# A fused attention and expert kernel whose hand-listed order of operations and loads is computed anew

## The chip, the cores and the metric

The kernel runs on one core of one Trainium2 chip. The metric is the device time of one execution in microseconds (us), as the median of several runs.

## What is computed

Eight batches of attention, eight heads each, 576 queries against 16 beacon keys and 576 causal keys of width 64, and then a gated feed-forward over the 4608 tokens that come out:

```python
scores = scale * np.matmul(q, k_all.transpose(0, 1, 3, 2))
scores = np.where(causal, -1000000000.0, scores)
...
x = np.ascontiguousarray(attn_out.transpose(0, 2, 1, 3)).reshape(B * S, H * D)
...
h = a * b @ w3          # a = x @ w1, b = x @ w2
return (h @ w_out).astype(np.float32)
```

Inputs and output are float32; the kernel works in float16 with float32 sums.

## The kernel before

There is no scheduler in the program. The string ORDER (L62 to L266) lists some 1,890 operations, and the last lines of the kernel walk through it and issue each one:

```python
for line in ORDER.split(";"):
    kind, *args = line.split()
    ops[kind](*(int(arg) if arg.isdigit() else arg for arg in args))
```

So the string sets the order in which each engine and each DMA queue gets its instructions, which PSUM bank an operation takes (its last numbers), whether DVE (D) or ACT (A) makes a copy, and which queue stores a result (P: GpSimd's, S: SyncE's). Each engine works its own instructions in order; between engines the semaphores of the program's tiles decide.

The names in ORDER, by stage. `b` is a batch, `t` a pair of heads, `c` a chunk of 128 rows.

- Loads. For batch 0, `lq` and `lk` (L396, SyncE's queue) bring q and k as float32 into the staging tiles `st`; for the others `lq` (L377), `lk` (L385) and `lv` (L385) bring chunks of q, k and v on GpSimd's queue, with a cast to float16; `lkb` (L410) and `lvb` (L418) bring the beacon rows. `l1`, `l2` (L423) load the first two expert weights into `w`, `l3` (L432) rows of the third into `st`, `lo` (L435) the output weight into `wo`.
- Transposes. For batches 0 to 2 (and with `x` for the attention outputs of batches 0 and 1) PE transposes (`tq`, `tk`, L451 and L457; `x`, L592). From batch 3 on `Dq` (L500) and `Dk` (L506) do it by a DMA on SyncE's queue, and so does `TX` (L601) for the attention output from batch 2 on: it writes xT from x.
- Attention. `s` (L535) makes a group of score blocks, `exp` (L545, ACT) their exponentials in `ring`, `m` (L555, DVE) the causal mask, `v` (L566) the product with the values, `n` (L577, L578, DVE) the division by the sum, into x.
- Fold of two weights. `t3` (L513) and `f` (L520) make Wt = w3 times w_out, `ew` copies it from PSUM. It is done once, between batch 0 and batch 1.
- Expert. Tokens of batch 0 go through plain products `a`, `b` (L660). For the other batches seven products `p` (L649) stand for the eight of a two by two block product; `S` (L618) are the sums of the halves of xT that they need and `T` (L631) those of the weights, on DVE. `ce`, `c1` (ACT, L678, L681), `u`, `t1`, `t2`, `g1`, `g2` (DVE, L684 to L698) put the products together and multiply a by b into gT.
- Output. `o` (L704) multiplies gT by Wt, `eo` (L358 on ACT, L360 on DVE) scales the sum into a staging tile `st`, and `st` (L717) stores it. There are eight staging tiles, so an `eo` waits until the earlier store from its tile has landed.

While the products of one batch run, the scores of the next but one are prepared. A sum S of a batch waits until the five transposes TX of that batch have landed; they wait for the last `n` of the batch. A load into a buffer waits for the last reader two batches earlier.

Of the kernel before, what the change touches and what calls it, by code (L numbers as in the profile page):

```python
# [68 lines left out]
cast 0 3 k; s 0 6 0; l1 1; m 0 1 1; tk 0 3 7; exp 0 6 0; cast 0 3 q; s 0 7 2; lq 1 4 P; m 0 0 1;
tq 0 3 6; exp 0 7 2; l1 0; eq 0 3 D 6; v 0 0 1 5; l3 1; ek 0 3 A 7; v 0 0 0 4; m 0 1 0;  # L70
n 0 0 1 5; l3 6; s 0 8 0; v 0 1 0 7; exp 0 8 0; l2 1; n 0 0 0 4; s 0 10 2; m 0 2 0; s 0 9 4;
exp 0 10 2; s 0 11 0; m 0 2 1; l2 0; v 0 1 1 6; n 0 1 0 7; exp 0 9 4; s 0 12 2; l2 3; n 0 1 1 6;
v 0 2 1 7; exp 0 11 0; m 0 3 0; t3 0 6; n 0 2 1 7; l1 2; v 0 2 0 5; exp 0 12 2; v 0 3 0 4;
m 0 3 1; tq 1 4 7; l1 3; n 0 2 0 5; e3 0 A 6 0; v 0 3 1 3; n 0 3 0 4; lq 1 3 P; tq 1 0 5;
n 0 3 1 3; x 0 0 4; x 0 4 6; tk 1 3 2; ex 0 0 A 4; eq 1 4 D 7; x 0 1 3; ex 0 4 A 6; l2 2;
x 0 3 1; ex 0 1 D 3; x 0 2 7; ex 0 3 A 1; t3 1 6; ex 0 2 D 7; a 0 3 1 7; lo 0; a 0 1 1 4;
a 0 3 0 3; ea 0 1 1 A 4 1; lo 1; b 0 3 0 1; ea 0 3 0 D 3 2; b 0 3 1 4; ea 0 3 1 D 7 0; a 0 0 0 3;
g 0 3 1 4 0; lk 1 4 P; b 0 0 0 7; T 1 1; ea 0 0 0 A 3 3; g 0 3 0 1 2; a 0 1 0 4; ek 1 3 A 2;
g 0 0 0 7 3; a 0 2 1 3; lk 1 2 P; T 0 1; ea 0 1 0 A 4 0; b 0 1 1 7; ea 0 2 1 A 3 2; a 0 2 0 4;
e3 1 A 6 1; g 0 1 1 7 1; lk 1 0 P; b 0 2 1 3; T 1 2; ea 0 2 0 A 4 3; b 0 2 0 7; b 0 1 0 6;  # L80
# [718 lines left out]
```

## Time and profile before

| what | us |
|---|---|
| median of 3 runs | 294.33 |
| all runs | 293.73, 297.48, 294.33 |
| the profiled execution, its own time | 293.03 |
| its span, first to last instruction | 291.3 |

The rows further down come from the one profiled execution. Times in them are microseconds from the span's start. PE is TensorE's matmul, PEld its weight load, DVE VectorE, ACT ScalarE, POOL GpSimd, SP SyncE; SPq is SyncE's sequencer, which issues DMAs. A line such as L649 is a line of the kernel.

### The profile page before, as it was taken

What the parts mean: (1) busy time and instruction counts of PE and PEld (TensorE: products, weight loads), DVE (VectorE), ACT (ScalarE), POOL (GpSimd) and SP (SyncE); (2) the same over time, 40 slices, a digit from 0 to 9 for tenths busy, and PEclk for the clock granted to TensorE, in tenths of its full rate; (3) what the DMA queues carried; (4) which work ended last, traced back from release to release, by engine and by line L of the source; (5) the groups of instructions that cost most, each with busy time, mean ns of one, the idle gap of its engine ahead of it and who ended that gap; (6) DMA issues with size and microseconds to landing.
All of it is one profiled execution on the core that took longest, in us unless ns stands there. A gap on an engine that the chain in (4) does not pass through costs nothing.

```text
span 291.3 us, 8145 instructions
## 1 busy us (share of the span) xinstructions
PE 276.5 (95%) x3204; PEld 185.4 (64%) x3204; DVE 227.7 (78%) x605; ACT 172.7 (59%) x272; POOL 133.5 (46%) x185
## 2 busy tenths in 40 slices
PE   6799999999999999998969998999999999999994
PEld 2478776657576756765647645775776667766751
DVE  5786785666799958996669867998899788997970
ACT  2686335857886489257954388434848886424313
POOL 8496696995982602959314570583500021002000
PEclk9579999999999999999999999999999999999999
DMA  7999999999999994999999999999992163602004
GB/s 199 205 186 199 187 170 182 174 143 128 108 145 134 115 128 81 170 160 177 175 148 115 157 140 227 73 134 184 218 192 44 40 146 104 124 2 108 38 0 180
DMA packets 156549, 40.33 MB, mean 138 GB/s; under 512 B 146208, under 2 KB 152864, under 8 KB 156512
## 3 DMA queue, kind: packets, MB, share of 16 engines
q0 software_dynamic: 114384, 26.62, 104.8%
q1 hardware_dynamic: 42128, 13.20, 28.9%
q8 instruction: 25, 0.41, 0.6%
q14 instruction: 12, 0.10, 0.1%
HBM read 39.32 MB, written 9.44 MB: 167 GB/s over the span
## 4 chain that ended last, share of the span: by engine, by line
PE 78%; DMA 10%; DVE 5%; POOL 2%; issue 2%; SPq 1%; ACT 1%; DVEq 0%; POOLq 0%; ACTq 0%
PE ps L649 30%; PE ps L704 17%; PE ps L535 8%; PE ps L566 8%; PE ps L660 5%; PE ps L520 5%; DMA xT<-x 3%; DMA out_dram<-st 3%; DMA kT<-k 2%; DMA b<-in_beacon_k_dram 2%; PE ps L457 1%; DVE x L578 1%; POOL q L377 1%; PE ps L451 1%; PE ps L513 1%
## 5 line engine op out<-in xcount | busy, mean ns | idle before, releaser
L545 ACT ACTIVATE ring<-ps 128x1024 f16<-128x1024 f32 x104 | 101.5, 1024 | 25.7 <-PE ps L535 24.0
L704 PE MATMUL ps<-Wt,gT 128*128 128x512 f16 x288 | 77.4, 380 | 0.0
L649 PEld LDWEIGHTS <-w 128*128 128x128 f16 x448 | 42.6, 98 | 17.7 <-issue 1.4
L678 ACT COPY es<-ps 128x288 f32<-128x288 f32 x56 | 22.2, 400 | 45.1 <-PE ps L649 39.4
L717 POOL DMA_DIRECT2D out_dram<-st x31 | 17.6, 577 | 62.8 <-ACT st L358 26.4
L649 PE MATMUL ps<-S,T 128*128 128x288 f16 x224 | 42.0, 286 | 2.3 <-DVE x L578 2.3
L649 PE MATMUL ps<-xT,w 128*128 128x288 f16 x224 | 43.0, 286 | 0.0
L649 PE MATMUL ps<-S,w 128*128 128x288 f16 x224 | 42.4, 286 | 0.2 <-DVE gT L698 0.2
L566 PEld LDWEIGHTS <-ring 128*128 128x128 f16 x960 | 35.5, 99 | 10.3 <-issue 2.2
L649 PEld LDWEIGHTS <-T 128*128 128x128 f16 x336 | 31.5, 98 | 15.3 <-issue 3.3
L566 PE MATMUL ps<-va,ring 128*128 128x65 f16 x960 | 38.9, 195 | 1.5 <-DMA va<-in_v_dram 1.3
L385 POOL DMA_DIRECT2D va<-in_v_dram x40 | 34.5, 871 | 12.4 <-PE ps L704 10.3
L535 PE MATMUL ps<-qT,kT 64*128 64x80 f16 (+4 forms) x736 | 36.2, 232 | 3.3 <-DVE kT L354 1.4
L385 POOL DMA_DIRECT2D k<-in_k_dram x35 | 30.0, 870 | 19.9 <-DMA kT<-k 10.0
L377 POOL DMA_DIRECT2D q<-in_q_dram x35 | 30.4, 878 | 16.3 <-DMA qT<-q 13.5
L704 PEld LDWEIGHTS <-gT 128*128 128x128 f16 x288 | 25.2, 98 | 18.4 <-issue 3.1
L535 PEld LDWEIGHTS <-kT 64*128 64x128 f16 x736 | 20.8, 97 | 21.5 <-issue 16.5
L578 DVE TENSOR_TENSOR x<-ps,rd 128x256 f16<-128x256 f32 (+1 forms) x64 | 31.4, 491 | 2.2
L698 DVE TENSOR_TENSOR gT<-ps,es 128x288 f16<-128x288 f32 x64 | 28.5, 451 | 4.7 <-PE ps L649 2.6
L684 DVE TENSOR_TENSOR us<-ps,es 128x288 f32<-128x288 f32 x56 | 25.1, 452 | 3.6 <-PE ps L649 3.0
L681 ACT COPY ps<-ps 128x288 f32<-128x288 f32 x56 | 21.3, 384 | 10.8 <-PE ps L649 8.1
L687 DVE TENSOR_TENSOR us<-ps,us 128x288 f32<-128x288 f32 x56 | 24.6, 451 | 2.8 <-PE ps L649 1.5
(69 smaller groups left out, 318.3 us busy)
## 6 DMA issues: line engine op xcount, KB each, us to landing
out_dram<-st POOLq DMA_DIRECT2D x31, 256.0 KB, 6.8
q<-in_q_dram POOLq DMA_DIRECT2D x28, 128.0 KB, 6.5
va<-in_v_dram POOLq DMA_DIRECT2D x24, 128.0 KB, 6.9
k<-in_k_dram POOLq DMA_DIRECT2D x21, 128.0 KB, 5.9
st<-in_moe_w_dram POOLq DMA_DIRECT2D x8, 256.0 KB, 7.0
w<-in_moe_w_dram POOLq DMA_DIRECT2D x8, 256.0 KB, 9.2
out_dram<-st SPq DMA_DIRECT2D x5, 256.0 KB, 2.3
st<-in_q_dram SPq DMA_DIRECT2D x4, 288.0 KB, 6.6
```

The costliest lines, as they stand in the source:

```text
L377: nc.gpsimd.dma_start(dst[:rows, c], src[b, :, ds(c * P, rows), :].rearrange("h s d -> s h d"))
L385: nc.gpsimd.dma_start(dst[ds(p0, rows), c], src[b, :, ds(s0, rows), :].rearrange("h s d -> s h d"))
L535: nc.tensor.matmul(pair(n)[:, hh, ds(col, w)], kT[ds(hh * 64, 64), t, ts(jt, P)], qT[ds(hh * 64, 64), t, ds(q0, w)],)
L545: nc.scalar.activation(held(b, g)[:, :, 0:GW], pair(n), AF.Exp, scale=scale)
L566: nc.tensor.matmul(pv[:, 2 * at + hh, 0 : D + 1], held(b, g)[:, hh, ds(col, P)], va[:, jt, 2 * t + hh, 0 : D + 1], start=(jt == 0), stop=( ...
L578: nc.vector.tensor_tensor(x16s[b % NB2][:, ds(2 * h, ni), ts(t, P)].rearrange("p i (h d) -> p i h d", h=2), pv[:, 0 : 2 * ni, 0:D].rearran ...
L649: nc.tensor.matmul(half(n), sta[:, j], mov[:, j], start=(j == 0 and i in (1, 3, 5)), stop=(j == 1), skip_group_check=True,)
L678: nc.scalar.copy(es[i], half(n))
L684: nc.vector.tensor_tensor(us[j], half(n), es[i], ALU.add)
L687: nc.vector.tensor_tensor(us[j], half(n), us[j], ALU.add)
L698: nc.vector.tensor_tensor(gT[:, kf, ds((2 * b + 1) % 4 * HT, HT)], half(n), es[i], ALU.mult)
L704: nc.tensor.matmul(bank(n), gT[:, kf, ds(i * P % NG2, P)], Wt[:, kf, :], start=(kf == 0), stop=(kf == NFT - 1),)
```

## The change

Only ORDER changes: all of its lines are written anew. Every kind of operation occurs as often as before (392 `p`, 144 `o`, 104 `s`, 64 `v`, 30 `TX`, 25 `Dq`, 25 `Dk`, 36 stores, of them 31 on GpSimd's queue), and no tile and no function is touched. PE and the two queues issue as many instructions as before; between DVE and ACT some copies change sides: 17 of the 36 `eo` are on DVE in place of 12, and 12 of the 28 copies of transposed q and k in place of 19. The fold moves up: 12 of the 32 `f` and 4 of the 8 `t3` now stand ahead of the first expert product of batch 0, where there were 2 `t3` and no `f`; the three `tq` and `tk` of batch 1 that stood there move behind it. The first lines below are around the transposes TX of batch 3, the others around the fold.

```diff
-st 4 P 4; m 4 1 0; o 10 1 0; TX 3 3; t2 1 0; exp 4 0 2; v 4 1 0 4; st 2 P 2; m 4 0 1; p 2 6 4 1;
-s 4 5 6; n 4 1 0 4; TX 3 1; s 4 7 2; exp 4 5 6; o 10 2 0; g2 2 6 1 0; m 4 0 0; o 9 3 5;
...
+exp 0 4 2; tq 0 3 1; t3 0 0; l3 1; exp 0 3 4; s 0 5 2; l3 6; exp 0 5 2; tk 0 3 5; m 0 1 0;
+e3 0 D 0 0; lo 1; ek 0 3 A 5; eq 0 3 D 1; l1 1; exp 0 7 6; v 0 0 1 0; m 0 2 0; m 0 1 1; lo 2;
...
+c1 0 6; o 9 2 1; TX 3 2; g2 2 5 4 1; p 2 7 4 5; p 2 6 6 6; g2 2 7 5 3; p 2 6 3 4; o 11 0 2;
+u 6 2 0; TX 3 4; o 11 1 2; t1 4 0; p 2 6 2 0; s 4 6 4; Dk 5 3; g1 2 6 0 0; o 10 2 7; exp 4 6 4;
```

Three places, as the engines' instructions stand. First SyncE's queue at the five transposes TX of batch 3 (xT_59 from x_1_78; qT_72 and kT_74 belong to batch 4, qT_73 and kT_75 to batch 5). Before:

```order
L506 DMA_TRANSPOSE kT_74<-k_0_68 128x4x128
L601 DMA_TRANSPOSE xT_59<-x_1_78 128x4x112
L601 DMA_TRANSPOSE xT_59<-x_1_78 128x4x80
L601 DMA_TRANSPOSE xT_59<-x_1_78 128x4x128 x3
L500 DMA_TRANSPOSE qT_73<-q_1_67 128x4x64
L500 DMA_TRANSPOSE qT_73<-q_1_67 128x4x128 x3
L506 DMA_TRANSPOSE kT_75<-k_1_69 128x4x128 x3
```

The five stood behind all transposes of batch 4 and ahead of those of batch 5. After:

```order
L506 DMA_TRANSPOSE kT_74<-k_0_68 128x4x128 x2
L601 DMA_TRANSPOSE xT_59<-x_1_78 128x4x128
L506 DMA_TRANSPOSE kT_74<-k_0_68 128x4x80
L601 DMA_TRANSPOSE xT_59<-x_1_78 128x4x128
L500 DMA_TRANSPOSE qT_72<-q_0_66 128x4x128
L601 DMA_TRANSPOSE xT_59<-x_1_78 128x4x112
L601 DMA_TRANSPOSE xT_59<-x_1_78 128x4x128
L601 DMA_TRANSPOSE xT_59<-x_1_78 128x4x80
L506 DMA_TRANSPOSE kT_75<-k_1_69 128x4x128
```

The last two transposes of batch 4 have moved between the first ones of x. Second, GpSimd's queue at the same place. Before, with 15 loads and stores listed between the first TX of batch 3 and the last (va is v, st the output staging tiles), its end:

```order
L377 DMA q_0_66<-in_q_dram 128x8x64 x2
L385 DMA va_71<-in_v_dram 128x8x64 x2
L717 DMA out_dram<-st_91 128x512
L717 DMA out_dram<-st_89 128x512
L410 DMA k_1_69<-in_beacon_k_dram 16x8x64
```

The store from st_89 stood between the third and the fourth TX. After, the five TX of batch 3 all stand between the first row here and the second, with no load or store listed between them:

```order
L385 DMA va_70<-in_v_dram 128x8x64
L717 DMA out_dram<-st_91 128x512
L385 DMA k_1_69<-in_k_dram 128x8x64
L385 DMA k_0_68<-in_k_dram 128x8x64 x2
L377 DMA q_1_67<-in_q_dram 128x8x64
```

The loads of batches 5 and 6 stand behind the transposes where they stood among them. Third, GpSimd's queue in the opening (st there is a row block of w3, wo the output weight, w the first two expert weights). Before:

```order
L385 DMA va_70<-in_v_dram 80x8x64
L377 DMA q_1_67<-in_q_dram 128x8x64
L432 DMA st_87<-in_moe_w_dram 128x1024
L385 DMA k_1_69<-in_k_dram 128x8x64
L423 DMA w_62<-in_moe_w_dram 128x4x256
L377 DMA q_1_67<-in_q_dram 64x8x64
L423 DMA w_62<-in_moe_w_dram 128x4x256
```

Here w stood ahead of wo, which followed behind all eight loads of w. After:

```order
L385 DMA va_70<-in_v_dram 128x8x64
L432 DMA st_87<-in_moe_w_dram 128x1024
L385 DMA va_70<-in_v_dram 128x8x64
L385 DMA va_70<-in_v_dram 112x8x64
L418 DMA va_70<-in_beacon_v_dram 16x8x64
L385 DMA va_70<-in_v_dram 128x8x64
L385 DMA va_70<-in_v_dram 80x8x64
L432 DMA st_89<-in_moe_w_dram 128x1024
L435 DMA wo_65<-in_moe_w_out_dram 128x2x512
```

One block of w3 has moved in behind the first chunk of batch 0's v, and wo ahead of w.

## Rows read from the trace of the kernel before

**Rows 1.** The page: span and busy time of the engines.

```profile
span 291.3 us, 8145 instructions
PE 276.5 (95%) x3204; PEld 185.4 (64%) x3204; DVE 227.7 (78%) x605; ACT 172.7 (59%) x272; POOL 133.5 (46%) x185
```

**Rows 2.** Stretches of 10 us: length, each engine's busy time (instructions), granted clock, DMA.

```profile
core 0: us, PE busy (x) PEld busy (x) DVE busy (x) ACT busy (x) POOL busy (x), PEclk, DMA share, GB/s
130.00:140.00 10.00, 9.08 (x123) 5.47 (x121) 6.54 (x19) 7.45 (x10) 10.00 (x14) 1.00 2.31 162
140.00:150.00 10.00, 7.67 (x129) 4.74 (x128) 5.90 (x16) 7.46 (x10) 0.61 (x2) 1.00 1.69 169
170.00:180.00 10.00, 8.62 (x141) 5.16 (x141) 5.96 (x16) 8.99 (x11) 3.58 (x6) 1.00 2.15 195
```

**Rows 3.** PE in order of time: start, length, instructions, [idle before <- releaser].

```profile
136.05 0.30 PE L566 MATMUL ps<-va,ring 128*128 128x65 f16 x4
136.61 0.19 PE L566 MATMUL ps<-va,ring 128*128 128x65 f16 x1 [0.26 <-DMA va<-in_v_dram]
137.45 0.37 PE L566 MATMUL ps<-va,ring 128*128 128x65 f16 x7 [0.66 <-DMA va<-in_v_dram]
...
149.37 0.41 PE L649 MATMUL ps<-S,T 128*128 128x288 f16 x2 [2.33 <-DVE x L578]
...
172.52 0.54 PE L566 MATMUL ps<-va,ring 128*128 128x65 f16 x12 [0.35 <-DMA va<-in_v_dram]
...
179.82 0.60 PE L535 MATMUL ps<-qT,kT 64*128 64x112 f16 x15 [1.02 <-DVE st L360]
```

**Rows 4.** The chain that ended last, pieces with their lengths.

```profile
139.09 8.95 DMA xT<-x
149.23 0.82 DVE S L618 x2
...
170.92 8.06 DMA out_dram<-st
179.08 0.70 DVE st L360
```

**Rows 5.** GpSimd's queue, 122 to 150 us, in order of time.

```profile
128.16 2.31 POOL L385 DMA_DIRECT2D k<-in_k_dram x3 [3.02 <-DMA kT<-k]
...
131.34 1.79 POOL L385 DMA_DIRECT2D va<-in_v_dram x2
...
139.39 1.22 POOL L717 DMA_DIRECT2D out_dram<-st x2
```

**Rows 6.** Issues of DMA, 130 to 150 us: median us to landing.

```profile
out_dram<-st POOLq DMA_DIRECT2D x3, 256.0 KB, 7.7
xT<-x SPq DMA_TRANSPOSE x3, 7.2
```

**Rows 7.** The same view of 222 to 256 us.

```profile
out_dram<-st POOLq DMA_DIRECT2D x7, 256.0 KB, 3.2
xT<-x SPq DMA_TRANSPOSE x10, 3.2
```

**Rows 8.** Line L601, the transposes TX, over the whole span.

```profile
DMA to landing us min/median/max: 2.3/4.4/9.6
```

**Rows 9.** The fold's group by line: count | busy us, mean ns of one.

```profile
L520 PE MATMUL ps<-wo,wT 128*128 128x512 f16 x64 | 16.8, 380 | 0.0
```

**Rows 10.** The opening in stretches, columns as in rows 2.

```profile
5.00:9.00 4.00, 1.57 (x26) 1.27 (x27) 2.27 (x4) 0.82 (x3) 4.00 (x6) 0.94 1.14 254
9.00:18.00 9.00, 7.59 (x105) 5.32 (x103) 7.20 (x13) 7.85 (x10) 4.87 (x8) 0.50 1.95 187
19.00:28.00 9.00, 8.38 (x177) 6.99 (x174) 7.02 (x22) 7.04 (x9) 6.21 (x9) 1.00 1.40 198
```

**Rows 11.** The end: the last matmuls and the last scaling copy.

```profile
282.51 4.76 PE ps L704 x22
...
287.30 0.60 ACT st L358
```

More of the change, by code (lines that the diff above doesn't have):

```diff
@@ L69 @@
[L69 to L80, printed above, removed]
@@ new lines @@
+n 0 3 0 7; f 1 1 6 2; lk 1 3 P; f 6 1 4 3; x 0 2 7; x 0 4 1; x 0 1 3; ex 0 2 A 7; ex 0 4 D 1;
+f 6 2 4 3; lq 1 1 P; ex 0 1 D 3; f 0 2 0 0; x 0 3 7; x 0 0 1; f 1 2 6 2; ex 0 3 A 7; lk 1 1 P;
+ex 0 0 D 1; f 1 3 6 2; a 0 3 0 7; ew 1 A 6; a 0 2 0 1; l1 2; a 0 1 1 6; b 0 2 0 3;
+ea 0 1 1 D 6 2; l2 2; b 0 1 1 2; ea 0 2 0 D 1 1; T 0 1; b 0 3 0 6; lv 1 4; g 0 1 1 2 2;
+f 2 2 5 1; g 0 2 0 3 1; a 0 3 1 2; ea 0 3 0 D 7 0; l3 7; a 0 0 0 3; ea 0 3 1 D 2 2; a 0 2 1 7;
+g 0 3 0 6 0; ea 0 0 0 A 3 1; T 0 2; b 0 2 1 2; lk 1 0 P; ea 0 2 1 A 7 3; b 0 3 1 6; lk 1 2 P;
@@ new lines @@
+t3 5 7; g 0 3 1 6 2; f 0 3 0 0; T 1 1; e3 5 A 7 2; lkb 1; b 0 0 0 6; T 0 4; f 2 3 5 1;
+g 0 0 0 6 1; l1 3; a 0 0 1 7; g 0 2 1 2 3; ew 2 A 5; t3 4 6; ea 0 0 1 A 7 0; b 0 0 1 5;
+e3 4 A 6 0; lq 1 2 P; a 0 4 0 7; g 0 0 1 5 0; tk 1 1 1; a 0 5 1 5; ek 1 1 D 1; lk 1 4 P;
+a 0 1 0 6; ew 0 D 0; ea 0 5 1 A 5 0; tq 1 4 1; ea 0 4 0 A 7 1; l2 3; b 0 5 1 3; ea 0 1 0 D 6 2;
+T 2 1; b 0 4 0 7; T 1 2; b 0 1 0 6; lq 1 0 P; eq 1 4 D 1; a 0 5 0 5; f 4 0 2 0; lq 1 3 P;
+ea 0 5 0 D 5 3; tq 1 1 1; g 0 5 1 3 0; f 4 1 2 0; lk 2 3 P; g 0 4 0 7 1; f 4 2 2 0; a 0 4 1 7;
@@ new lines @@
+lk 2 0 P; b 0 5 0 5; ea 0 4 1 A 7 0; t3 7 3; l3 3; f 6 3 4 3; e3 7 D 3 1; lv 1 3; b 0 4 1 7;
+g 0 5 0 5 3; tk 1 2 0; lv 1 2; a 0 7 1 3; g 0 4 1 7 0; ew 6 D 4; tk 1 4 5; tq 1 2 7; ek 1 4 A 5;
+lv 1 1; f 4 3 2 0; ea 0 7 1 D 3 1; tk 1 0 4; eq 1 1 A 1; ew 4 D 2; b 0 7 1 5; lq 2 4 P;
+eq 1 2 A 7; tk 1 3 3; ek 1 2 D 0; tq 1 0 2; ek 1 0 A 4; T 3 1; a 0 7 0 7; lkb 2; ek 1 3 A 3;
+g 0 7 1 5 1; tq 1 3 4; a 0 6 1 1; eq 1 0 A 2; eq 1 3 D 4; lk 3 2 P; f 5 0 5 2; g 0 1 0 6 2;
+ea 0 6 1 A 1 3; s 1 5 2; ea 0 7 0 A 7 0; lv 1 0; s 1 0 0; exp 1 5 2; s 1 1 6; f 7 0 4 1;
@@ new lines @@
+t1 7 0; p 3 2 2 3; p 3 0 5 6; Dq 5 0; u 5 1 1; p 3 1 3 7; ce 6 2; g1 3 2 3 0; p 3 0 1 2;
+p 3 1 7 5; t1 7 1; c1 2 6; p 3 3 5 3; t2 5 1; p 3 3 1 1; Dk 5 0; ce 3 3; p 3 0 6 6; g1 3 1 0 1;
+p 3 1 4 5; c1 1 3; u 6 2 0; p 3 0 2 2; p 3 0 3 7; g2 3 1 5 1; p 3 0 7 6; p 3 3 6 3; t1 7 0;
+TX 4 2; p 3 3 3 5; t2 6 2; p 3 5 5 7; p 3 5 1 0; u 3 3 1; ce 7 1; p 3 0 4 6; g1 3 0 2 0;
+p 3 2 7 4; Dk 5 1; c1 0 7; p 3 3 7 3; g2 3 0 6 2; p 3 3 2 1; t1 5 1; p 3 5 6 7; p 3 4 5 6;
+t2 4 0; p 3 5 2 0; u 7 1 0; ce 6 2; p 3 4 1 2; TX 4 3; p 3 2 4 4; t2 3 3; c1 2 6; o 14 0 5;
@@ new lines @@
+g1 3 3 1 1; p 3 4 6 6; g2 3 2 4 0; p 3 4 2 2; Dq 5 4; u 6 2 1; p 3 5 3 1; p 3 4 3 4; t1 1 0;
+o 14 1 5; TX 4 4; lkb 7; t1 4 1; p 3 4 7 6; p 3 5 7 7; g1 3 5 0 0; lv 5 0; o 13 0 4; TX 4 0;
+g1 3 4 2 1; p 3 7 5 1; t2 6 2; p 3 3 4 3; lv 5 2; ce 1 0; t2 7 1; p 3 7 1 0; p 3 4 4 6;
+g2 3 3 3 3; TX 4 1; c1 0 1; o 14 2 5; lq 6 4 P; g2 3 4 6 2; p 3 7 6 1; p 3 5 4 7; lv 6 1;
+u 1 0 0; p 3 7 3 6; p 3 6 5 3; g2 3 5 7 1; Dq 6 1; p 3 7 7 1; ce 3 2; t1 6 0; p 3 6 1 2; lv 6 2;
+p 3 7 2 0; t2 1 0; c1 2 3; s 5 1 6; g1 3 7 0 0; p 3 7 4 1; lk 6 0 P; Dq 6 0; exp 5 1 6;
@@ new lines @@
+n 5 0 1 4; eo 16 A 5 6; s 5 8 0; s 5 12 2; m 5 3 1; st 11 P 3; exp 5 8 0; s 5 10 4; o 17 1 6;
+S 4 2; o 17 2 6; exp 5 10 4; m 5 2 1; p 4 0 5 1; o 17 3 6; n 5 1 1 7; lq 7 2 P; exp 5 12 2;
+Dk 6 3; p 4 0 1 0; v 5 2 1 5; eo 17 D 6 0; lq 7 4 P; o 15 0 7; ce 1 0; n 5 2 1 5; v 5 3 1 6;
+c1 0 1; Dq 6 2; lk 7 1 P; S 4 4; s 5 9 2; S 4 3; s 5 6 4; lq 6 3 P; exp 5 9 2; p 4 0 6 1;
+n 5 3 1 6; Dk 6 2; p 4 0 2 0; o 15 1 7; u 1 0 0; lk 6 4 P; exp 5 6 4; p 4 0 3 6; m 5 3 0;
+p 4 3 5 3; t1 6 0; p 4 3 1 2; lvb 6; Dk 6 0; p 4 0 7 1; ce 3 1; m 5 2 0; v 5 3 0 6; st 16 P 6;
@@ new lines @@
+p 5 1 5 4; S 5 4; v 6 2 0 3; S 5 3; lq 7 0 P; ce 4 1; o 21 3 6; eo 20 A 0 0; n 6 2 0 3;
+p 5 0 6 7; eo 21 A 6 3; lq 7 3 P; v 6 0 0 2; u 7 0 0; p 5 1 1 1; n 6 0 0 2; p 5 4 5 6; c1 1 4;
+lv 7 0; p 5 0 7 7; p 5 0 3 0; ce 6 2; t2 7 0; p 5 4 1 3; p 5 1 6 4; t1 0 0; st 13 P 5; c1 3 6;
+p 5 0 4 7; u 4 1 1; p 5 0 2 5; st 12 P 4; p 5 1 3 2; g2 5 0 7 0; p 5 4 6 6; t1 2 1; p 5 4 3 0;
+p 5 1 7 4; u 6 2 2; p 5 1 2 1; st 21 P 3; t2 4 1; p 5 4 7 6; p 5 2 5 7; t1 0 2; p 5 2 1 2;
+t2 6 2; lv 7 3; ce 7 0; p 5 4 2 3; p 5 1 4 4; g1 5 1 1 1; c1 2 7; p 5 4 4 6; g1 5 4 3 2;
@@ new lines @@
+p 5 5 5 1; lv 7 2; Dk 7 3; p 5 5 1 0; g2 5 4 6 2; ce 1 3; p 5 2 6 7; g1 5 0 5 0; p 5 7 5 6;
+c1 0 1; p 5 7 1 3; u 7 0 1; lv 7 1; ce 6 2; p 5 2 3 5; g2 5 1 4 1; p 5 5 6 1; c1 3 6; p 5 2 2 2;
+t1 5 1; st 20 P 0; p 5 2 7 7; Dq 7 3; p 5 7 6 6; g1 5 2 2 1; s 6 3 4; st 15 P 1; t2 7 0;
+p 5 7 2 3; u 1 3 0; exp 6 3 4; p 5 5 3 2; Dk 7 2; u 6 2 1; p 5 5 2 0; p 5 5 7 1; t1 2 0;
+p 5 2 4 7; t2 1 3; p 5 7 3 5; p 5 7 7 6; g2 5 2 7 0; p 5 3 5 4; Dq 7 0; t1 5 1; p 5 3 1 2;
+ce 4 1; p 5 5 4 1; t2 6 2; p 5 6 5 7; c1 2 4; g1 5 7 3 1; p 5 6 1 5; ce 7 0; p 5 7 4 6;
@@ new lines @@
+p 6 4 1 1; u 5 2 1; p 6 0 4 6; c1 1 7; p 6 1 7 4; t1 3 0; p 6 1 2 2; TX 7 1; g2 6 0 6 0;
+p 6 3 7 5; p 6 4 6 7; g1 6 1 2 0; p 6 2 5 6; t2 4 1; p 6 2 1 3; ce 6 0; p 6 4 2 1; t2 5 2;
+TX 7 4; p 6 3 3 2; c1 3 6; u 7 3 0; p 6 1 4 4; p 6 3 4 5; t1 2 1; p 6 3 2 0; TX 7 3; g2 6 3 5 2;
+p 6 2 6 6; p 6 2 2 3; g1 6 3 0 1; p 6 4 3 5; u 6 0 2; p 6 4 7 7; p 6 6 5 2; t1 5 0; p 6 6 1 0;
+ce 2 2; g2 6 1 4 1; p 6 2 7 6; p 6 2 3 5; g1 6 4 1 0; c1 0 2; o 27 0 4; t1 5 2; p 6 6 2 0;
+t2 6 0; p 6 6 6 2; p 6 5 5 5; g1 6 2 3 2; p 6 2 4 6; t2 7 3; ce 5 1; p 6 5 1 1; o 27 1 4;
@@ new lines @@
+g2 6 2 6 0; c1 1 5; p 6 4 4 7; u 2 2 0; p 6 7 5 6; g2 6 4 7 3; p 6 5 6 5; ce 6 0; p 6 7 1 3;
+u 5 1 1; p 6 5 3 7; c1 3 6; p 6 5 2 1; t1 7 1; p 6 6 7 2; p 6 7 6 6; g1 6 5 1 1; p 6 5 7 5;
+p 6 6 3 7; u 6 0 2; o 29 0 1; S 7 1; p 6 7 7 6; t1 7 0; o 27 2 4; g1 6 6 0 0; o 29 1 1; t2 5 1;
+p 6 7 3 7; o 28 0 0; S 7 2; t1 7 2; p 6 7 2 3; o 28 1 0; t2 6 0; p 6 5 4 5; g1 6 7 3 2;
+p 6 7 4 6; t2 2 2; o 28 2 0; S 7 3; o 27 3 4; g2 6 5 5 1; p 7 4 5 7; g2 6 7 6 0; o 28 3 0;
+ce 7 3; eo 27 D 4 0; p 7 4 1 3; p 7 3 5 6; c1 3 7; p 6 6 4 2; o 29 2 1; ce 6 0; g2 6 6 2 2;
@@ L267 @@
+t2 5 1; p 7 5 2 4; p 7 7 4 6; g2 7 5 7 2; p 7 6 4 5; g2 7 7 6 3; p 7 6 2 1; o 34 2 3; g2 7 6 5 1;
+p 7 5 3 7; o 35 2 0; t1 7 1; o 35 3 0; g1 7 5 4 1; o 34 3 3; eo 35 A 0 0; o 31 0 7; eo 34 D 3 1;
+o 32 1 2; p 7 6 3 6; st 34 S 1; o 33 0 3; t1 6 0; st 35 S 0; o 32 2 2; g1 7 6 1 0; o 33 1 3;
+o 33 2 3; o 32 3 2; o 33 3 3; eo 32 A 2 1; o 31 1 7; eo 33 D 3 0; st 32 S 1; o 31 2 7; o 31 3 7;
+st 33 S 0; eo 31 A 7 2; st 31 S 2
 """
```

325 lines of the change are left out of this document (135 added, 190 removed).

## The prediction

> **What bounds the kernel now.** I read the page's busy times first, then the stretches of 10 us, then PE in order of time where a stretch is not full, and last the chain and the two queues at those places.
>
> PE is busy for 276.5 of 291.3 us [rows 1]; no other engine comes near. The change leaves every matmul in the program, so what it can win is PE's idle time and what the low clock of the opening costs, and nothing else. After the opening PE is short of work in three stretches of 10 us only: it is idle for 10.00 - 9.08 = 0.92 us from 130 on, 2.33 from 140 on and 1.38 from 170 on [rows 2], 4.63 us in all.
>
> PE in order of time says where [rows 3]. The 0.92 are two waits for values of batch 4 (0.26 and 0.66). The 2.33 end at 149.37, before the first product of batch 3. The 1.38 are 0.35 for values of batch 5 and 1.02 for a DVE copy into a staging tile.
>
> Who is late is read from the chain, not from the releaser beside the idle time. "DVE x L578" at 149.37 is only DVE's last instruction before the one that mattered: the chain has a transpose that took 8.95 us to land and then the sums S [rows 4]. And the copy L360 at 179.08 followed a store that took 8.06 us: the copy writes the staging tile that this store had yet to read out. So all four are late landings. The loads were issued late: GpSimd's queue stood for 3.02 us until a transpose of k had landed that was to read the buffer first, so the values of batch 4 were issued at 131.34, and PE asked for them at 136.05 [rows 3, 5].
>
> How long a landing takes depends on what else is on the way. From 130 to 150 us, where both queues issue, a transpose TX takes 7.2 us in the median and a store 7.7 [rows 6]; from 222 to 256 us, where GpSimd's queue has only stores, both take 3.2 [rows 7]. Over the whole span a TX takes between 2.3 and 9.6 us [rows 8].
>
> **The change part by part.** The sum is made against the profiled execution, 293.03 us; the median of the runs shown, 294.33, is 1.30 above it, and I carry the differences over to the median as they are.
>
> *The sums of batch 3.* In the list, PE had 152 matmuls between the last division of batch 3 and its first sum S (2 of L649, 18 of L704, 78 of L566, 54 of L535); now it has 202, and 104 of these are the large products of L649. That stretch was too short for three transposes in a row at 7 to 9 us each to land. Besides, the five TX stand where GpSimd's queue has nothing listed, so the 3.2 us of [rows 7] is the nearer row to expect, not the 7.2 of [rows 6]. The wait of 2.33 goes; at worst none of it does. I take -2.33.
>
> The rule that speaks against the whole term is that a queue which goes quiet frees nothing until what it issued has landed, and the trace agrees: the 8.95 us landing began at 139.09, when the last loads of the burst were being issued [rows 4, 5]. The Trainium skill's page "DMA: Bandwidth & Descriptors", section "Issuing engines are not separate DMA queues", says that DMAs of all issuing engines run on the same 16 DMA engines and interleave there. By that rule alone, with the number of bytes unchanged, the transposes would still meet the loads and the term would be 0, which makes the sum 2.33 less.
>
> *The values of batches 4 and 5.* The last chunk of v for batch 4 stood 98 matmuls ahead of its first use; now 140, of which 84 are large. No transposes of k that are still on their way stand ahead of these loads. -0.92 and -0.35, bounds 0 and these.
>
> *The staging tile at 179 us.* The store and the copy into the same tile are now paired in another way; the copy of output tile 16 goes to ACT and to a staging tile from which nothing was stored before. -1.02, bounds 0 and this. Together the waits after the opening are worth -4.62 (4.63 less rounding), and 0 if all come back.
>
> *The fold moved up.* 24 matmuls of L520 now stand ahead of the first expert product. At 16.8/64 = 0.26 us each [rows 9] that is 6.3 us of PE's work, taken from later stages, where PE is full, into the opening, where it is not. It is no work less; its worth is the idle time that it fills. From 19 to 28 us PE is idle for 9.00 - 8.38 = 0.62 us and ACT's exponentials fill the time; from 9 to 18 us it is idle for 1.41 [rows 10]. The fold needs w3 and wo, which are listed behind the values of batch 0, so the second stretch is the one it can fill. I take -0.62; the bounds are 0 and -2.03.
>
> *Copies between DVE and ACT.* Five output copies come to DVE at 0.70 us [rows 4], 3.5 us; seven copies of q and k leave it. DVE is idle for 22% of the span [rows 1], so this costs nothing so long as no stretch is full; where DVE is full, it would cost those 3.5 us at most.
>
> *New waits.* Every landing now stands behind another operation, and no trace shows the new pairs. From below they cost 0; from above, a tile whose store takes 8.06 us again [rows 4] behind a stretch that hides none of it. The nearest row is a wait for a landing that was nearly in time, 0.66 [rows 3]. I take +0.66.
>
> *The end.* The last 22 matmuls run without a gap and one scaling copy of 0.60 us follows [rows 11]; the new list ends in the same way, four last products, one copy on ACT, one store. 0.
>
> Sum: -4.62 - 0.62 + 0.66 = -4.58. On the profiled execution that gives 288.4, on the median 294.33 - 4.58 = 289.75, or 1.6% less.
>
> **The rivals.** A difference of 2%, 5.9 us, is about what a measurement of this kernel can tell from no change.
>
> *All of the waiting goes, and the opening gains too.* -4.62 - 2.03 = -6.65, which is 287.7. For it: the fold is work that waits for neither q nor k nor v. Against it: ACT's exponentials, not PE, set the pace from 9 to 28 us (ACT is busy for 7.85 and 7.04 of 9 us [rows 10]), and the new list gives ACT two more copies there.
>
> *Batch 2 takes the place of batch 3.* Between the last division of batch 2 and its first sum PE had 174 matmuls, 44 of them large; now it has 156, 2 of them large. The last three TX of that batch stand right behind a run of loads. If they land in the 8.95 us of [rows 4], and not in 3.2, DVE stands at the sum as it did at 149 us, and the same 2.33 us come back. With two such places, -4.62 - 0.62 + 0.66 + 2.33 gives -2.25, which is 292.1. For it: what is before those transposes is just what was before the late ones. Against it: only two or three loads are listed right ahead.
>
> *Slower: the opening stays at the low clock.* Place: 9 to 28 us. The granted clock was 0.94 from 5 to 9 us, with PE busy for 1.57 of 4 us, then 0.50 from 9 to 18 us (1.2 of 2.4 GHz) with 7.59 of 9, and 1.00 from 19 on [rows 10]. A block of w3 now comes ahead of most of v, and PE reaches the values in order, with the fold queued behind them. If PE then has gaps in the stretch that brought the clock up, it stays at 1.2 GHz for as long again: 8.38 us of PE's work from 19 to 28 us would take twice the time. The exponentials hide part; half of it costs 4.2, all of it 8.4, in the middle +6.3. That decides once it is over the 4.6 us of waits saved: 294.33 - 4.62 + 6.3 = 296.0. For it: the opening is the one stretch where PE has gaps already. Against it: the new list has more matmuls there, not fewer.
>
> *The list does not do what it says*: a margin is given in a planner's time, and the queues may run otherwise. Then the four waits come back at other places, and the time is that of before, 294.3.
>
> **How the numbers follow.** My forecast of 289.75 gets 0.42, with a range of its own from 288.0 to 291.5. The full gain, 287.7, gets 0.25; batch 2 (292.1) 0.14; the list that does not do what it says (294.3) 0.09; slower (296.0) 0.10. The limit for faster by over 2% is 288.4: four fifths of the full gain's chance lie under it and a third of the forecast's, 0.20 + 0.14 = 0.34. The limit for slower by over 2% is 300.2; only the whole 8.4 us with waits come back reaches it: 0.04. The rest, 0.62, is within 2%. For 8 in 10 the range goes from 286.0 (the full gain, with 1.7 for where a clock that rises sooner would add to it) to 296.0.
>
> **What would show it right or wrong.** In the new profile, PE should have no idle time of over 0.7 us after 30 us, DVE no wait before a sum L618 of batch 3, and the TX of that batch should land in some 3 us. The first product of the fold should start before 25 us, with PE at 1.00 of its clock from 19 us on. I am wrong if PE's idle time after 30 us is still above 3 us, if L618 of batch 2 waits for xT for more than 1 us, or if the clock stays at 0.50 beyond 22 us. If the waits go and the time does not fall by 4 us, the work was limited by something that no stretch of PE shows as idle.

## The result, and the profile after

The changed kernel took 285.19 us in the median (284.45 to 286.17), the old one beside it 294.03; the ratio is 0.972, with an interval from 0.967 to 0.977. The forecast was 289.75, with a range from 286.0 to 296.0: the gain was there, and it was larger than any case I gave. Ratios here leave out executions more than 1.5% above the fastest of their kernel; medians and ranges take all. Over all runs of this study the old kernel's 56 executions have a median of 293.08, from 290.2 to 301.4 (292.56 for the 38 that the ratios keep), and the new one's 8 a median of 285.19, from 284.5 to 286.7.

The profiled execution of the new kernel took 286.17, so the two profiles differ by 6.86 us. The page's head, for [rows 1]:

```profile
span 284.2 us, 8158 instructions
PE 274.5 (97%) x3204; PEld 185.6 (65%) x3204; DVE 229.3 (81%) x606; ACT 170.8 (60%) x271; POOL 133.4 (47%) x185
```

The stretches, first of the opening, for [rows 10], then around the old waits, for [rows 2]. The columns are length, busy time of each engine (instructions), granted clock, DMA share and GB/s:

```profile
5.00:9.00 4.00, 2.30 (x39) 1.58 (x37) 2.78 (x5) 1.22 (x3) 3.37 (x5) 1.00 1.22 263
9.00:18.00 9.00, 8.11 (x118) 6.03 (x119) 6.27 (x14) 8.25 (x12) 5.81 (x9) 0.62 1.63 200
19.00:28.00 9.00, 9.00 (x159) 6.57 (x156) 5.92 (x18) 6.53 (x8) 4.83 (x8) 1.00 1.29 202
...
130.00:140.00 10.00, 9.77 (x113) 5.05 (x112) 7.66 (x20) 7.40 (x9) 5.20 (x7) 1.00 0.94 127
140.00:150.00 10.00, 10.00 (x173) 7.47 (x171) 9.27 (x27) 8.46 (x14) 4.30 (x6) 1.00 1.88 159
170.00:180.00 10.00, 8.84 (x138) 6.30 (x135) 8.08 (x22) 6.52 (x10) 6.80 (x10) 1.00 2.65 193
```

From 19 to 28 us PE has no gap left, and in the three stretches around the old waits one wait of over 0.3 us is left, at 170 to 180. PE in order of time, for [rows 3]: the first matmuls of the fold, the first expert product, and that one wait:

```profile
20.80 0.59 PE L520 MATMUL ps<-wo,wT 128*128 128x512 f16 x2
...
30.02 1.27 PE L660 MATMUL ps<-xT,w 128*128 128x288 f16 x9
...
174.92 0.71 PE L566 MATMUL ps<-va,ring 128*128 128x65 f16 x18 [1.16 <-DVE st L360]
```

It is none of the four old ones; the chain there has the pattern of [rows 4] with other tiles: a copy on DVE waits for a store that still reads its staging tile.

```profile
165.97 8.11 DMA out_dram<-st
174.17 0.70 DVE st L360
```

At the sums of batch 3, GpSimd's queue (for [rows 5]) stood idle until 134.81, and the five TX between 122 and 136 us, in the view of DMA issues (for [rows 6]), landed in 4.0 us in the median:

```profile
134.81 0.58 POOL L717 DMA_DIRECT2D out_dram<-st  x1 [14.92 <-DVE st L360]
```

```profile
xT<-x SPq DMA_TRANSPOSE x5, 4.0
```

One measure more is used below, an estimate: what PE has lost at a point, which is the time less the work ahead of it, each operation at its length from start to start where nothing holds it up (0.43 us for a group of two fold matmuls, 0.45 for the transposes of a block of w3, 0.245 for a product p). Ahead of the first expert product the new list has 5.49 us more work than the old: 12 groups of the fold and two blocks of w3, less three transposes of batch 1. It starts that product at 30.02. The old one did so at 27.22, as a row of PE in order of time of the kernel before says:

```profile
27.22 3.96 PE L660 MATMUL ps<-xT,w 128*128 128x288 f16 x31 [0.16 <-DVE xT L354]
```

So the new list comes there 2.80 later with 5.49 more done, and is 2.69 ahead. Behind that product the old list loses 10.15 us in its profile, the new one 6.03, and 4.44 in a second profile of it. The first two differ by 4.12; with the 2.69 of the opening that is 6.81 of the 6.86 us.

### The profile page after: what moved, and what is told of

It reads as the page before. It is cut to its first block, busy times and chain, and to the rows that moved or that the text cites. A ratio compares the mean times of both kernels' runs of the same rounds, so it can differ in the third digit from the quotient of the medians.

```text
span 284.2 us, 8158 instructions
## 1 busy us (share of the span) xinstructions
PE 274.5 (97%) x3204; PEld 185.6 (65%) x3204; DVE 229.3 (81%) x606; ACT 170.8 (60%) x271; POOL 133.4 (47%) x185
## 4 chain that ended last, share of the span: by engine, by line
PE 85%; DMA 7%; DVE 3%; ACT 2%; issue 1%; SPq 1%; POOL 0%; DVEq 0%
PE ps L649 33%; PE ps L704 19%; PE ps L566 9%; PE ps L535 8%; PE ps L660 6%; PE ps L520 5%; DMA out_dram<-st 3%; DMA st<-in_q_dram 2%; DMA xT<-x 2%; PE ps L457 2%; PE ps L513 1%; ACT ring L545 1%; PE ps L592 1%; DVE st L360 1%; SPq L396 1%
## 5 line engine op out<-in xcount | busy, mean ns | idle before, releaser
L545 ACT ACTIVATE ring<-ps 128x1024 f16<-128x1024 f32 x104 | 99.9, 1032 | 23.2 <-PE ps L535 22.5
L678 ACT COPY es<-ps 128x288 f32<-128x288 f32 x56 | 23.0, 410 | 45.1 <-PE ps L649 38.6
L649 PE MATMUL ps<-xT,w 128*128 128x288 f16 x224 | 43.8, 286 | 0.0
L649 PE MATMUL ps<-S,T 128*128 128x288 f16 x224 | 42.6, 286 | 0.0
L566 PEld LDWEIGHTS <-ring 128*128 128x128 f16 x960 | 34.8, 97 | 10.1 <-issue 2.8
L535 PE MATMUL ps<-qT,kT 64*128 64x80 f16 (+4 forms) x736 | 34.4, 230 | 1.6 <-DVE kT L354 0.7
L385 POOL DMA_DIRECT2D k<-in_k_dram x35 | 29.9, 867 | 12.7 <-DMA kT<-k 7.2
L578 DVE TENSOR_TENSOR x<-ps,rd 128x384 f16<-128x384 f32 (+1 forms) x64 | 31.4, 491 | 2.2
```

Of the source, the lines that this page charges most:

```text
L385: nc.gpsimd.dma_start(dst[ds(p0, rows), c], src[b, :, ds(s0, rows), :].rearrange("h s d -> s h d"))
L535: nc.tensor.matmul(pair(n)[:, hh, ds(col, w)], kT[ds(hh * 64, 64), t, ts(jt, P)], qT[ds(hh * 64, 64), t, ds(q0, w)],)
L545: nc.scalar.activation(held(b, g)[:, :, 0:GW], pair(n), AF.Exp, scale=scale)
L566: nc.tensor.matmul(pv[:, 2 * at + hh, 0 : D + 1], held(b, g)[:, hh, ds(col, P)], va[:, jt, 2 * t + hh, 0 : D + 1], start=(jt == 0), stop=( ...
L578: nc.vector.tensor_tensor(x16s[b % NB2][:, ds(2 * h, ni), ts(t, P)].rearrange("p i (h d) -> p i h d", h=2), pv[:, 0 : 2 * ni, 0:D].rearran ...
L649: nc.tensor.matmul(half(n), sta[:, j], mov[:, j], start=(j == 0 and i in (1, 3, 5)), stop=(j == 1), skip_group_check=True,)
```

## The experiments

**Which part of the list wins.** Both lists hold the same operations, so one can be followed up to a point and the rest taken from the other in its own order. Cut points are where no PSUM bank has to change. The seams, at the first product with the values (16 us) and at 60 us:

```diff
 front16_new: new order up to
+ek 0 3 A 5; eq 0 3 D 1;
 then what is left of the old
-lq 1 0 P; lk 1 3 P; l1 1; m 0 1 1; lq 1 4 P; exp 0 7 6; l1 0; v 0 0 1 5;
 open60_old: old order up to
-s 1 11 0; lk 3 0 P; s 1 9 6; exp 1 11 0; f 3 0 3 3; lk 2 0 P; f 5 2 5 2; exp 1 9 6;
 then what is left of the new
+f 4 3 2 1; ew 4 D 2; lq 2 4 P; lkb 2; lk 3 2 P; f 7 1 4 0; f 7 2 4 0;
```

> The old order for the first 60 us, the new one behind. If what the new order wins behind 60 us (4.1 us of PE's waits in the traces) does not depend on when the opening ends, 285.2 + 2.7 = 287.9. If the times of the landings in the middle hang on the opening, waits of over 1 us show up that the new trace does not have, and it is 289 or more.

It took 287.77 (287.57 to 288.80), a ratio to the old kernel of 0.983 (0.977 to 0.989); its repetition on another chip (below) 288.20, a ratio of 0.983 (0.973 to 0.993). So the new order behind 60 us is worth some 5 us, and the opening 2.6 to 3.0 (against 285.2, which the new kernel took in other rounds). This is the sum's two halves apart, and the opening is where the forecast fell furthest short: it had 0.62.

> The old order up to the first product with the values of batch 0, the new one behind. Theory 1: 285.2 + 2.2 = 287.4. Theory 2: 285.7 or less.

290.80 (290.16 to 295.96), 3 us above open60_old, so neither theory: the old first 16 us and the new rest do not fit. PE in order of time shows the seam: a block of w3 and the output weight, which the old front had not yet loaded.

```profile
24.30 0.62 PE L513 MATMUL ps<-ident,st 128*128 128x128 f16 x8 [1.05 <-DMA st<-in_moe_w_dram]
25.57 0.59 PE L520 MATMUL ps<-wo,wT 128*128 128x512 f16 x2 [0.64 <-DMA wo<-in_moe_w_out_dram]
```

> The new order up to the first product with the values of batch 0 (some 16 us), behind it the old order. Theory 1 (the opening gains in its first 16 us, by an earlier start of the exponentials and a clock that rises sooner): 1.1 us are won at that product and 1.1 more because the products behind it run at full clock, so 294.0 - 2.2 = 291.8, and the granted clock is 1.00 from 17 us on. Theory 2 (the fold that was moved up fills idle time of PE, as I had it in the prediction): the first 16 us are worth less than 0.5, so 293.5 or more.

296.96 (295.21 to 297.89): slower than the old kernel, by a ratio of 1.013 (1.006 to 1.020). The same misfit the other way round: w3 and the output weight had gone ahead, and a transpose of batch 1, early in the old order, waited 1.89 us for its load.

```profile
27.59 0.30 PE L457 MATMUL ps<-ident,q 64*128 64x64 f16 x4 [1.89 <-DMA q<-in_q_dram]
```

> The new order for the first 60 us (opening, fold, most of batch 0's products), the old one behind. Both theories: 294.0 - 2.7 = 291.3, since PE lost 2.7 us less before 60 us in the new trace than in the old; the waits at 137, 149, 172 and 180 us come back, some 2.7 us earlier. By the difference to the run with 16 us: theory 1 less than 0.6, theory 2 about 2.

297.04 (293.17 to 301.31), a ratio of 1.008 (1.002 to 1.013). Its opening is as good as the new one's (first expert product at 30.20), but the seam adds waits for DVE of 2.85 us between 61 and 65. The profile is of the slowest of its ten executions, 301.31, so the size of its waits is not that of the median. The run says nothing on the size of the opening; of the old rest it shows how far its waits can move:

```profile
150.88 0.41 PE L649 MATMUL ps<-S,T 128*128 128x288 f16 x2 [1.63 <-DVE x L578]
183.99 1.01 PE L535 MATMUL ps<-qT,kT 64*128 64x112 f16 x15 [4.21 <-DVE st L360]
```

In the old kernel's profile these two are 2.33 and 1.02 [rows 3].

**What wins the opening.** First the fold is moved back in the new list (two groups take another PSUM bank):

```diff
-e3 2 D 7 1; f 0 0 0 0; ... f 2 0 5 1; e3 1 A 6 2; ... t3 6 7; f 0 1 0 0; ...
 a 0 3 0 7;
+f 0 0 0 0; t3 1 6; f 2 0 5 1; a 0 2 0 1; e3 1 A 6 2; t3 6 2; f 0 1 0 0; e3 6 A 2 3; f 1 0 6 2;
```

> The new order with the fold moved back: two transposes of w3 ahead of the first expert product as in the old order, the other two and the 12 groups of the fold in between the first products. Theory fold (PE's gaps between 16 and 30 us are filled by it): the gaps come back, 1.0 to 1.6 us behind the first product with the values, 0.6 behind the last: 285.2 + 2.0 = 287.2. Theory start (the gain is the earlier start of the exponentials and the sooner rise of the clock): at most 0.6 comes back, 285.8 or less.

292.88 (292.41 to 293.24): 7.65 more than the new kernel on the same chip, all of its gain and nearly four times what I expected from the fold. PE in order of time, and stretches of 1 or 2 us:

```profile
25.03 0.54 PE L566 MATMUL ps<-va,ring 128*128 128x65 f16 x12 [1.15 <-DVE ring L555]
26.30 2.04 PE L592 MATMUL ps<-ident,x 128*128 128x128 f16 x20 [0.73 <-DVE x L578]
28.92 1.12 PE L660 MATMUL ps<-xT,w 128*128 128x288 f16 x4 [0.57 <-DVE xT L354]
```

```profile
25.00:26.00 1.00, 0.54 (x12) 0.45 (x13) 0.36 (x2) 0.00 (x0) 0.01 (x1) 1.00 1.37 197
26.00:27.00 1.00, 0.70 (x11) 0.70 (x11) 0.25 (x1) 0.25 (x1) 0.53 (x1) 0.76 1.36 202
30.00:31.00 1.00, 1.00 (x6) 0.47 (x4) 0.00 (x0) 0.00 (x0) 0.56 (x1) 0.50 1.67 194
32.00:34.00 2.00, 2.00 (x15) 1.27 (x14) 0.00 (x0) 0.79 (x1) 1.48 (x2) 0.66 1.45 189
```

Without the fold the gaps are there. After the one that ends at 26.30 the granted clock falls to 0.50, and until 33.3 us PE's matmuls run at half rate (the products L660 start 0.24 us apart there, and 0.12 from 35 us on), so some 3 us of the loss are the clock. The fold's new place has waits of its own, 0.24 at 35.07 and 0.67 at 40.83. Between 20 and 50 us this list loses 8.4 us, the new one 0.4. The run shows gaps, clock and new place together and does not part them.

Then the other theory alone, in the old list:

```diff
-lq 0 0 S; consts 0; lk 0 0 S; lq 0 1 S; consts 3; spin 8 7; consts 2; ... consts 1; lk 0 3 S; lkb 0;
+lk 0 0 S; consts 0; lq 0 0 S; lq 0 1 S; consts 3; spin 8 7; consts 1; lkb 0; consts 2;
-cast 0 0 q; lv 0 3; cast 0 0 k; ... s 0 1 0; cast 0 1 k; tn 0 7; tq 0 1 6; lv 0 4; en 0 A 7;
+cast 0 0 k; lv 0 3; cast 0 0 q; ... tn 0 7; en 0 A 7; ... s 0 1 0; cast 0 1 k; tq 0 1 6; lv 0 4;
```

> The old order with only the first 9 us changed: k of batch 0 loaded and cast ahead of q, the beacon keys loaded ahead of the masks, and their transposes ahead of the first scores. Theory start: the first exponential begins at 8.0 in place of 8.9 us, and the time falls by 0.9 to 1.1, to some 292.1 (by the 293.1 of before's 19 runs). Theory fold: the exponentials start earlier too, but without work to fill the gaps less than 0.4 of it is seen at the end: 292.7 or more.

293.48 (292.07 to 295.08), a ratio to the old kernel of 1.006 (1.000 to 1.013). The first product with the values did come 0.83 us sooner, at 16.31, but at the first expert product, 26.99, only 0.23 of it was left, and the end saw none. Theory start falls for the old list. Its waits behind are here of another size: there is none before batch 3's first product, and those of [rows 3] at 172 and 180 have grown.

```profile
168.76 0.54 PE L566 MATMUL ps<-va,ring 128*128 128x65 f16 x12 [0.72 <-DMA va<-in_v_dram]
177.34 1.01 PE L535 MATMUL ps<-qT,kT 64*128 64x112 f16 x15 [2.31 <-DVE st L360]
```

Last, the fold by itself moved into the old opening, with the new rest behind 60 us (seven groups take another bank):

```diff
 s 0 9 4;
+t3 0 6; exp 0 10 2; s 0 11 0; l2 1; m 0 2 1; e3 0 A 6 0;
 v 0 1 1 6;
+f 0 0 3 0; ... t3 1 2; ... e3 1 A 2 1; v 0 2 1 7; f 0 1 3 0; f 1 0 6 1; ...
```

> open60_old (old order for the first 60 us, new behind) with the fold moved up inside the old opening: 12 groups of the fold and three transposes of w3 stand among the products with the values of batch 0, the blocks of w3 and the output weight are loaded ahead of the first two expert weights, and three transposes of batch 1 move behind the first expert products. Theory fold (moving the fold up is what wins the opening, by itself): PE has lost some 10 us at the first expert product in place of 13, and the time is 2 to 2.7 under open60_old, some 285.5. By the term in the prediction: 0.6 under it. Theory together (the fold pays only with the rest of the new opening): no gain, or worse, because a load of w3 is late again as in front16_old.

> open60_old once more, as the base on the same chip for the run beside it: 287.8 within 0.5, with executions within 2 us of each other.

294.41 (293.79 to 296.79) against 288.20 (287.44 to 289.04): 6.2 us slower than its base. Theory fold falls: moving the fold up does not win by itself. "Together" had this outcome, but not its reason, since no wait of PE from 19 us on names a load of w3. PE in order of time, of the profile of open60_old and then of this kernel:

```profile
27.71 3.47 PE L660 MATMUL ps<-xT,w 128*128 128x288 f16 x27 [0.16 <-DVE xT L354]
```

```profile
22.64 0.70 PE L566 MATMUL ps<-va,ring 128*128 128x65 f16 x18 [1.08 <-ACT wT L354]
...
34.55 1.63 PE L660 MATMUL ps<-xT,w 128*128 128x288 f16 x12 [0.61 <-DVE xT L354]
...
56.31 0.41 PE L535 MATMUL ps<-qT,kT 64*128 64x112 f16 x12 [1.11 <-ACT ring L545]
57.23 0.40 PE L535 MATMUL ps<-qT,kT 64*128 64x112 f16 x12 [0.51 <-ACT ring L545]
```

At the first expert product it is 6.84 us later with some 5.04 more done (12 groups of the fold and a block of w3, less three transposes of batch 1), so 1.8 us of the loss lie ahead of it. For these the rows name a cause. ACT in order of time of this kernel:

```profile
21.57 1.02 ACT L354 COPY wT<-ps 128x1024 f16<-128x1024 f16 x1
22.46 1.06 ACT L545 ACTIVATE ring<-ps 128x1024 f16<-128x1024 f32 x1
24.69 1.01 ACT L354 COPY wT<-ps 128x1024 f16<-128x1024 f16 x1 [1.17 <-PE ps L513]
25.60 1.03 ACT L545 ACTIVATE ring<-ps 128x1024 f16<-128x1024 f32 x1
26.85 1.01 ACT L354 COPY wT<-ps 128x1024 f16<-128x1024 f16 x1 [0.22 <-PE ps L513]
27.76 1.03 ACT L545 ACTIVATE ring<-ps 128x1024 f16<-128x1024 f32 x1
```

and of the new one:

```profile
17.56 3.92 ACT L545 ACTIVATE ring<-ps 128x1024 f16<-128x1024 f32 x4
21.76 1.94 ACT L545 ACTIVATE ring<-ps 128x1024 f16<-128x1024 f32 x2 [0.29 <-PE ps L535]
23.59 1.94 ACT L354 COPY wT<-ps 128x1024 f16<-128x1024 f16 x2
```

My list put three copies of w3's transposes between the exponentials, and the last of these starts at 27.76. The new list gives the first two copies to DVE, and ACT makes the other two, from 23.59 on, when its last exponential is done. So there the fold took turns on the engine that sets the pace.

The larger part, some 4.4 us, is lost behind that product: at the first product p, with the same work ahead of it in both lists, this kernel is at 91.53 us and open60_old at 85.32. Of PE's waits there the longest, at 56.31 and 57.23, are for exponentials of batch 1, three of whose transposes my list had moved behind the first products and some of whose loads behind those of w3 and the output weight. No run parts this from the copies.

**The late landings.**

```diff
-lk 6 2 P; n 3 2 0 6; ... lk 6 4 P; ... lk 5 4 P; ... lq 6 0 P; ... lv 4 2; ... lv 4 3;
+lv 4 2; lv 4 3; lk 6 2 P; n 3 2 0 6; ... lk 6 4 P; ... lk 5 4 P; ... lq 6 0 P;
```

> The old order; the last two loads of v of batch 4 stand ahead of the three loads of k on GpSimd's queue that wait for a transpose (3.02 us). The waits of 0.26 and 0.66 at 136 to 138 us go, since the values land by some 131 us. If nothing else is late, 0.9 less, 292.1 or so; if the 2.33 behind them only grow by what is won (PE comes earlier to sums that come no earlier), 0.

292.75 (292.12 to 298.51), a ratio of 1.003 (0.999 to 1.006). The values of batch 4 landed by 133.1 in place of 137.4 and their two waits went, but later ones stayed, at 1.28 before batch 3's first product and 1.35 at 178 us in this profile. A gain of 0.9 would be a ratio of 0.997, which the interval leaves out: taken away alone, in the old list, these two waits won nothing, as the second half of the expectation had it.

```diff
-lk 6 3 P; ... lkb 6; ... lq 6 1 P; ... lq 6 2 P; ... lv 5 3; ... lv 5 1; ... st 4 P 4;
 st 4 P 4; ... st 2 P 2; ... lkb 7;
+lk 6 3 P; lkb 6; lq 6 1 P; lq 6 2 P; lv 5 3; lv 5 1;
```

> The old order; six loads of batches 5 and 6 (k, q, v), which GpSimd's queue issued from 133.6 to 139.4 us, stand behind its next wait, at 152 us. Theory landing (the transposes TX of batch 3 were late because they met these loads): the last three of them land in 3 to 4 us in place of 5.9 to 9.0, PE does not wait ahead of the first product of batch 3, and the median falls by 2.3, to some 290.5. Rival lead (the stretch between the last division and the sum is too short, whatever is on the way): the wait stays over 1.5 and the time within 1. Where the old order's waits differ between executions, the profile may show others in their place.

298.61 (297.50 to 299.29), a ratio of 1.023 (1.016 to 1.029), some 6.5 us slower, and yet it shows the mechanism. The three TX issued between 136 and 142 us landed in 2.5 us in the median, and there is no wait before batch 3's first product. What was put off was late in its turn:

```profile
xT<-x SPq DMA_TRANSPOSE x3, 2.5
```

```profile
166.54 0.35 PE L535 MATMUL ps<-qT,kT 64*128 64x80 f16 x10 [3.22 <-DMA qT<-q]
174.58 0.54 PE L566 MATMUL ps<-va,ring 128*128 128x65 f16 x12 [1.73 <-DMA va<-in_v_dram]
```

The reverse, in the new list:

```diff
+lk 6 1 P; lk 5 1 P; lk 6 2 P; lq 5 3 P; lq 6 0 P; lq 6 1 P;
 st 9 P 4;
-... lk 5 1 P; ... lk 6 1 P; ... lk 6 2 P; ... lq 5 3 P; ... lq 6 0 P; ... lq 6 1 P;
```

> The new order; the six loads that stood behind the transposes TX of batch 3 on GpSimd's queue are issued ahead of a store, from 129.6 us on, and so meet the last three of these transposes. Theory lead (202 matmuls ahead of the sum hide even a late landing): the three land in 6 to 9 us in place of 2.5 to 4.6, and the time stays within 0.5 of 285.2. Theory landing: the sum S at 138.9 waits, PE stands 1 to 2.5 us at the first product of batch 3, and the time is 286.2 to 287.7.

287.99 (286.81 to 290.91), 2.8 above the new kernel's 285.2 of other rounds and just above the range that theory landing gave. The three TX issued from 129 to 134 us took 6.0 us in the median, and the last landed at 140.04 in place of 137.22. DVE stood 1.24 us at the sum, and 1.35 at a copy whose store had been pushed behind the loads (it took 8.0 us, 3.4 before):

```profile
xT<-x SPq DMA_TRANSPOSE x3, 6.0
```

```profile
140.17 0.83 DVE L618 TENSOR_TENSOR S<-xT 128x576 f16<-128x576 f16 x2 [1.24 <-DMA xT<-x]
...
142.98 0.69 DVE L360 TENSOR_SCALAR st<-ps 128x512 f32<-128x512 f32 x1 [1.35 <-DMA out_dram<-st]
```

Theory landing holds: 202 matmuls of lead alone did not hide the landing among six loads.

**The wait that is left.**

> The new kernel itself once more, as the base for the runs beside it and for a second profile: 285.2, with executions within 2 us of each other, where the old kernel's lie within 10 (291.1 to 301.4 in 19). If the wait of 1.16 us for a staging tile at 175 us is chance, it is gone or of another size in this profile.

285.23 (284.57 to 286.71), a ratio to the old kernel of 0.979 (0.973 to 0.984), after 0.972 in the first measurement. The wait at 175 us is not in this profile: the same store landed in 5.70 us, not 8.11.

```diff
-eo 17 D 6 0; ... st 17 P 0;
+eo 17 D 6 7; ... st 17 P 7;
```

> The new order; the DVE copy of output tile 17 and its store use the eighth staging tile, in which nothing was stored. If the 1.16 us that PE stood at 174.9 us came from the store that still held the other tile, the wait goes, with nothing late behind it: 1.2 us less than new_again. Rival: the wait differs from execution to execution, and the median of new_again holds little of it: less than 0.4.

284.93 (284.64 to 285.24): 0.30 less than new_again, which four executions of each do not tell apart. The rival holds; the highest time is 285.24 where the new order's is 286.71, which fits a wait that comes only in some executions, and is too little to show it.

```diff
-tq 0 1 7; ... eq 0 1 A 7;
+tq 0 1 7; ... eq 0 2 D 6; eq 0 1 D 7;
```

> new_tile7 with one copy of q of batch 0 on DVE, behind its other copy of q, in place of ACT. PE's gap of 0.36 to 0.54 us at 12.7 to 13.3 us goes. Theory start: the exponentials behind it come 0.5 earlier and the clock rises sooner: 284.4. Theory fold (what PE does not do in the opening it does later at full rate, so only idle time counts): the same 0.4 to 0.5 less, by the gap alone. Neither: ACT has its next exponential at the same time, no change, 284.9.

285.68 (285.11 to 286.22): nothing won. The gap went from 12.7 us and came back as waits of 0.52 at 15.71 and 0.58 at 16.70, for an exponential and for a copy on DVE.

```profile
15.71 0.41 PE L451 MATMUL ps<-ident,gT 96*128 96x96 f16 x6 [0.52 <-ACT ring L545]
```

These six transposes run at full rate, where six in the new kernel's profile still take 0.66 us at 14.02. So here the clock had risen sooner, and the time was not lower. No version here clearly beats the new kernel.

## Why the prediction was wrong

**The fold moved up** is the step that failed: "I take -0.62; the bounds are 0 and -2.03". The opening gave 2.69 in the profiles, more than even the bound, and 2.6 to 3.0 by open60_old. I took the idle time that the rows list from 19 to 28 us, 0.62, as all that could be filled; counted from start to start, the old list loses 1.5 us from 19 us to its first product, and the new one 0.1. That is 1.4. The other 1.3 lie ahead of 19 us, which I had left out of the sum: the first product with the values came at 16.49 in place of 17.14 with a block of w3 (0.45) more done. How much of these 1.3 is the clock, 0.62 in place of 0.50 from 9 to 18 us, no run shows. By old_front_early an earlier start alone leaves 0.23 at the first expert product; by new_fold_late the new front without the fold loses more than the old one did; by old60_fold_early the fold without the new front loses too. So the term belongs to the opening as a whole. And I priced gaps only, not what gaps can do to the clock: some 3 us of new_fold_late's 7.65 are the stretch at half rate. I had that mechanism, as the slower rival, and the argument against it ("the new list has more matmuls there, not fewer") was the right one, but I did not count it as a gain.

**The waits after the opening**, -4.62, went as forecast. For the sums of batch 3 the reason given is shown: the TX landed in 4.0 us where GpSimd's queue issued almost nothing beside them, and old_burst_late and new_burst_early show it both ways. For the values it is not shown that their waits are worth something by themselves (old_v_early), and the pairing of store and copy at 179 us was not tested alone. The term was too small, because idle time in the rows is less than what PE loses: the twelve matmuls of v at 136.05 to 137.82 [rows 3] take 0.54 us where nothing holds them up (the row at 172.52), so 1.23 was lost, not 0.92. From start to start the four waits come to 5.4. The Trainium skill's page "DMA: Bandwidth & Descriptors", section "Issuing engines are not separate DMA queues", says that DMAs of all issuing engines interleave on the same 16 engines; both runs agree, in which transposes TX took 2.5 or 6.0 us with GpSimd's queue quiet or busy. It did not make the term 0: the new list's loads stand where no wait for them is left, while in old_burst_late they were late in their turn, and it cost some 6.5 us.

**New waits**, +0.66: 1.16 in the profile of the result, 0.97 at the same place in that of open60_old_2, none there in those of new_again and open60_old. So it comes in two of these four profiles.

**The rivals.** Batch 2 did not take the place of batch 3: its last TX landed in 2.5 to 5.1 us, by 107.4, and no wait stands there. The list does what it says. The full gain was the right case, and too small by 2.5: with 5.4 for the waits and 2.7 for the opening the sum is 8.1, and the medians of 56 and 8 executions differ by 7.9 (7.4 with the 38). The base was high by chance: 294.33 was the median of three, 1.25 above that of the 56, so against the latter the forecast missed by 3.3 us and not by 4.6.

**The signs I named.** PE at 1.00 from 19 us on, the first fold product before 25, no wait at the sums of batch 3: all three came. The TX of batch 3 landed in 4.0 us where I had said some 3. "No idle time of over 0.7 us after 30 us" failed at 174.92; PE's waits listed after 30 us are 1.4 us in all, under the 3 that would have made me wrong.

## What to carry to other kernels

Price an idle engine by what it loses from start to start, at its full rate, and not by the gaps that the profile lists; where its clock falls behind a gap, as at 26 us in new_fold_late, the work that fills the gap is worth more than the gap. Independent work that is moved into gaps brings its helpers along (here copies and two weights' loads) and pushes other work back: look for the turns that the helpers take on the engine that sets the pace, and for who waits for what was pushed back. A transfer can land late because of what is issued beside it (2.5 and 6.0 us here): before it is given a margin, look for where the loads that made it late will go.
